# Spectral mixing with two channel networks on one core: two buffers for the first batch's second products, weight conversion as a list of operations, one group fewer multiplied unfolded, first pairs in two parts

## The chip, the cores and the metric

The kernel runs on 1 core of one Trainium2 chip. A core has five engines that run side by side, each with its own queue of instructions: TensorE (PE; matrix products), VectorE (DVE), ScalarE (ACT), GpSimd (POOL) and SyncE (SP), whose queue here only issues DMA transfers. ScalarE issues some too. The metric is the device time of one execution in microseconds (us); lower is better.

## The reference

Three layers follow each other on x of 4 batches x 3136 tokens x 256 channels, in fp32. The first is a filter along the sequence in the frequency domain; the second adds to its input the real part of a two-dimensional Fourier transform, and then a normalised two-layer network; the third is a network of the same kind with a gain.

```python
X = np.fft.rfft(x, axis=1)                      # first layer
x = np.fft.irfft(X * (filt_r + 1j * filt_i), n=3136, axis=1)
u = x + np.real(np.fft.fft(np.fft.fft(x, axis=1), axis=2))
un = (u - mean(u)) / np.sqrt(var(u) + 1e-6)     # second layer, over channels
x = u + np.maximum(un @ w1a, 0) @ w2a           # 256 -> 1024 -> 256
xn = (x - mean(x)) / np.sqrt(var(x) + 1e-6) * g # third layer
out = x + np.maximum(xn @ w1b, 0) @ w2b
```

## The kernel before

A sequence of 3136 is treated as 64 x 49: a transform of length 64 (`over_p`), one of length 49, the filter, and both back (`over_q`, 9 pairs j of frequency steps per batch). The channel transform is multiplied in when a block of tokens is prepared (`prep_ticks`). There are 25 blocks U of 512 tokens (the last 256); each goes through two network layers, and each layer is 8 steps m: `w1_step` (first product, 12 matrix instructions), `w1_evict` (ScalarE writes the high part `hh`, VectorE the low part `hl`), and `w2_step` (second product, 12 instructions). The products are exact to fp32 because each operand is split into a high and a low part and three products are added; so each weight has a high and a low part in SBUF.

The weights come as 64-bit words and are converted on the core, in chunks of 512 columns. A chunk goes through: load W (SyncE), masks E (two VectorE operations), value V (one, VectorE), scale A (two, ScalarE), join M (two, VectorE), high part H (ScalarE), low part L (VectorE). The first two chunks (w1a) are list A, tiles `we`; fourteen others are list Z, tiles `wm`, the first four of them w2a[0], w1a[1], w1a[3], w2a[1]. `conv_ticks` cuts this into ticks, with four chunks in work at a time.

The order of everything ahead of the first network step is written by hand: in `PLAN` each letter runs a tick of one stream (q: first batch's loop; a, c: conversion A and Z; p: preparation of block 0; x: x of batch 1; 0 to 3 and W to Z: transform of a group of batch 1, and its eviction). Behind that, `at` holds for each network step what runs in it, and `CONV` how many conversion ticks. An engine's queue is filled in the order of the code, and an engine executes it in that order; so an operation that waits holds up all behind it on its engine.

The loop of the first batch: for each j TensorE transposes g (L419) and multiplies (L251) into two banks R and I, VectorE multiplies them with the filter (first products y, L459; second products t2, L456), GpSimd adds the two (L461, L462) and forms z (L471, L472), TensorE transforms back (L251) and transposes (L506, L509), ScalarE evicts `vst` and `zt` and stores `vst`. Tile t2 has one buffer. Block 0's mixing begins on TensorE with the last `vst` (L659); it needs the whole loop. x of batch 1 is loaded in groups c of 512 KB. Groups 0 to 3 are multiplied whole (`whole_p`, 8 products of 512 columns on quarters of the array), the others are folded first: GpSimd forms sum and difference (L295, L296), 4 products follow (`over_p`).

Of the kernel before, what the change touches and what calls it, by code (L numbers as in the profile page):

```python
# [169 lines left out]
def spectral_mlp_kernel(ctx: ExitStack, tc, x, ff, cst, w1a, w2a, gln, w1b, w2b, out):  # L170
# [223 lines left out]
    def over_q(b):  # L394
# [32 lines left out]

        def into(j):
            g = g_raw.pop((b, j))
            R, I = (bank(2) for _ in range(2))  # L430
            f2 = const("f2")
            if j == 0:
                for r, o, n in ((0, R, "f2a"), (64, I, "f2a")):
                    quarter(o[:, 0], 0, const(n), r, NI, g[:, 0])
                for r, o, n in ((0, I, "f2b"), (64, R, "f2b")):
                    quarter(o[:, 0], 64, const(n), r, NI, g[:, 0])
# [343 lines left out]
    def conv_ticks(specs, bufs, when, lo_eng):  # L780

        chunks = []
        for n, j in specs:
            words = {"1a": w1a, "2a": w2a, "1b": w1b, "2b": w2b}[n].bitcast(I32).rearrange("p (n t) -> p n t", t=2)
            chunks.append((words, n, 512 * j))
        n = len(chunks)
# [2 lines left out]
        def load(t):
            for i in range(n):  # L790
                if when(i) != t:
                    continue
                words, _, a = chunks[i]
                ww[i] = bufs("w", i).bitcast(I32).rearrange("p (n t) -> p n t", t=2)
                nc.sync.dma_start(out=ww[i], in_=words[:, a:a + 512])

        load(-1)
        yield
        for t in range(n + LAG):
            load(t)  # L800
            i = t - LAG
            if i >= 0:
                _, name, a = chunks[i]
                dh, dl = (weight(name)[:, s].rearrange("p a b -> p (a b)") for s in range(2))
                conv_done.add(specs[i])
                split(vs.pop(i), dh[:, a:a + 512], dl[:, a:a + 512], lo_eng(i))
                yield
            i = t - 2
            if 0 <= i < n:
                p, v, w = ps.pop(i), vs[i], ww.pop(i)  # L810
                nc.vector.scalar_tensor_tensor(out=p, in0=w[:, :, 1], scalar=-0x80000000, in1=p,
                                               op0=ALU.bitwise_and, op1=ALU.bitwise_or)
                nc.vector.tensor_tensor(out=v, in0=v, in1=p.bitcast(F32), op=ALU.mult)
            i = t - 1
            if 0 <= i < n:
                nc.scalar.activation(out=ps[i], in_=ps[i], func=ACTF.Relu, scale=8.0, bias=-896.0 * 2 ** 23)
                nc.scalar.activation(out=vs[i], in_=vs[i], func=ACTF.Copy, scale=2.0 ** -20, bias=1.0)
            if 1 <= t <= n + 1:
                yield
            if t < n:  # L820
                low, high = ww[t][:, :, 0], ww[t][:, :, 1]
                e, m = (bufs(k, t).bitcast(I32) for k in "em")

                ps[t], vs[t] = e, m.bitcast(F32)
                nc.vector.tensor_single_scalar(out=e, in_=high, scalar=0x7FF00000, op=ALU.bitwise_and)
                nc.vector.tensor_single_scalar(out=m, in_=high, scalar=0xFFFFF, op=ALU.bitwise_and)
                yield
                nc.vector.scalar_tensor_tensor(out=vs[t], in0=low.bitcast(U32), scalar=2.0 ** -32, in1=m,
                                               op0=ALU.mult, op1=ALU.add)
                yield  # L830
# [338 lines left out]
```

## Time and profile before

| | us |
|---|---|
| median of 3 runs | 1345.01 (1344.9 to 1345.49) |
| profiled execution | 1344.32 |
| its span | 1342.5 |
| TensorE busy in the span | 1309.5 (98%) |
| VectorE, ScalarE, GpSimd busy | 783.9, 606.5, 257.6 |

The span is from the first to the last instruction of the profiled execution. Busy time of TensorE includes instructions that are in flight side by side, and their ends are modelled, so a busy TensorE may still lose time; its granted clock stands beside it. DMA moved 144.01 MB.

### The profile page before, as it was taken

The page shows a single profiled execution, that of the slowest core. Times are in us where ns is not written, and L with a number is a line of the kernel's source. Part 1 is how long each engine was busy: PE and PEld are TensorE (multiplying, and loading weights), DVE is VectorE, ACT ScalarE, POOL GpSimd, SP SyncE. Part 2 cuts the span into 40 slices and gives each one's busy share as a digit, 9 for nine tenths or more (in the row PEclk, how much of TensorE's full clock was granted, in tenths as well). Part 3 has the DMA queues.
Part 4 walks back from the last instruction along what each step waited for, and adds up shares of the span by engine and source line. Part 5 has one row for each costly group of instructions (what it writes and reads, how often), then busy time and mean ns, then how long its engine had stood idle before and what let it go on. Part 6 is the DMA issues. An engine that isn't in the chain of part 4 may idle for free.

```text
span 1342.5 us, 27955 instructions
## 1 busy us (share of the span) xinstructions
PE 1309.5 (98%) x11383; PEld 1213.0 (90%) x11383; DVE 783.9 (58%) x1633; ACT 606.5 (45%) x1142; POOL 257.6 (19%) x306
## 2 busy tenths in 40 slices
PE   7888999999999999999999999999999999999998
PEld 6467797989989989999989999999999999999998
DVE  5757775666555666656464665655545555565353
ACT  5455453454435444544435544545434543444222
POOL 2610202342230322212131231312000000000000
PEclk9988999999999999999999999999999999999999
DMA  7870222352544634623543635534222413432200
GB/s 246 308 245 17 67 86 83 117 164 81 149 130 133 159 91 113 170 53 95 129 132 106 165 104 119 151 82 107 56 64 48 95 41 71 79 85 43 63 17 25
DMA packets 209000, 144.01 MB, mean 107 GB/s; under 512 B 159196, under 2 KB 182492, under 8 KB 208872
## 3 DMA queue, kind: packets, MB, share of 16 engines
q1 hardware_dynamic: 192456, 112.20, 32.6%
q10 hardware_dynamic: 16416, 30.02, 5.9%
q8 instruction: 90, 1.47, 0.5%
q14 instruction: 38, 0.31, 0.1%
HBM read 83.08 MB, written 59.11 MB: 106 GB/s over the span
## 4 chain that ended last, share of the span: by engine, by line
PE 91%; DVE 4%; DMA 2%; ACT 1%; POOL 1%; issue 1%; SPq 0%; ACTq 0%; DVEq 0%
PE ps L869 40%; PE ps L842 39%; PE ps L251 7%; PE ps L664 3%; DMA fc<-in_ff 1%; PE ps L514 1%; PE ps L771 1%; DMA gd<-gst 1%; DVE t L456 1%; DVE y L459 1%; DMA ww<-in_w1a 0%; POOL y L462 0%; ACT xn L736 0%; DMA xr<-in_x 0%; PE ps L659 0%
## 5 line engine op out<-in xcount | busy, mean ns | idle before, releaser
L852 DVE SCALAR_TENSOR_TENSOR hl<-ps,hh 128x512 fp32r<-128x512 f32 (+1 forms) x400 | 269.7, 675 | 326.9 <-ACT hh L851 320.2
L851 ACT ACTIVATE hh<-ps 128x512 fp32r<-128x512 f32 (+1 forms) x400 | 233.9, 587 | 373.9 <-PE ps L869 330.6
L842 PE MATMUL ps<-xth,w1a 128*128 128x256 f32 x1568 | 244.9, 278 | 0.0
L842 PE MATMUL ps<-xth,w1b 128*128 128x256 f32 x1568 | 242.7, 276 | 0.0
L869 PE MATMUL ps<-w2a,hh 128*128 128x256 f32 x1568 | 220.8, 283 | 7.1 <-DVE w2a L248 4.0
L869 PEld LDWEIGHTS ps<-w2a,hh 128*128 128x128 f32 x1568 | 194.8, 189 | 35.8 <-issue 25.6
L869 PE MATMUL ps<-w2b,hh 128*128 128x256 f32 x1568 | 215.3, 279 | 0.0
L842 PEld LDWEIGHTS ps<-xth,w1a 128*128 128x128 f32 x1568 | 209.8, 189 | 1.4 <-ACT gst L359 1.4
L842 PEld LDWEIGHTS ps<-xth,w1b 128*128 128x128 f32 x1568 | 207.7, 188 | 0.0
L869 PEld LDWEIGHTS ps<-w2b,hh 128*128 128x128 f32 x1568 | 193.5, 188 | 13.7 <-issue 12.9
L719 POOL TENSOR_TENSOR rs<-rs,mhalf 128x4 f32<-128x4 f32 (+1 forms) x51 | 51.6, 1012 | 592.9 <-DVE rs L718 520.8
L842 PE MATMUL ps<-xtl,w1a 128*128 128x256 f32 x784 | 155.4, 278 | 0.0
L842 PE MATMUL ps<-xtl,w1b 128*128 128x256 f32 x784 | 154.2, 276 | 0.0
L730 ACT ACTIVATE xn<-u,nb,rs 128x256 f32<-128x256 f32 x148 | 117.1, 840 | 45.4 <-DVE nb L723 45.1
L869 PE MATMUL ps<-w2a,hl 128*128 128x256 f32 x784 | 122.5, 278 | 0.0
L869 PE MATMUL ps<-w2b,hl 128*128 128x256 f32 x784 | 121.6, 276 | 0.0
L842 PEld LDWEIGHTS ps<-xtl,w1a 128*128 128x128 f32 x784 | 119.7, 189 | 0.6 <-DVE xtl L765 0.6
L842 PEld LDWEIGHTS ps<-xtl,w1b 128*128 128x128 f32 x784 | 118.7, 188 | 0.0
L869 PEld LDWEIGHTS ps<-w2a,hl 128*128 128x128 f32 x784 | 104.8, 189 | 0.0
L869 PEld LDWEIGHTS ps<-w2b,hl 128*128 128x128 f32 x784 | 103.9, 188 | 0.0
L873 DVE TENSOR_TENSOR u<-ps,u 128x512 f32<-128x512 f32 x98 | 63.1, 684 | 44.0 <-PE ps L869 44.0
L461 POOL TENSOR_TENSOR y<-y,t 128x512 f32<-128x512 f32 (+1 forms) x35 | 43.5, 1243 | 148.8 <-DVE y L459 148.8
(133 smaller groups left out, 1422.1 us busy)
## 6 DMA issues: line engine op xcount, KB each, us to landing
xd<-xn SPq DMA_DIRECT2D x37, 512.0 KB
xtl<-xd SPq DMA_DIRECT2D x148, 128.0 KB
vd<-vst ACTq DMA_DIRECT2D x28, 512.0 KB
fc<-in_ff SPq DMA_DIRECT2D x26, 512.0 KB
vr<-vd SPq DMA_DIRECT2D x48, 256.0 KB
out<-u SPq DMA_DIRECT2D x24, 512.0 KB
xr<-in_x SPq DMA_DIRECT2D x18, 512.0 KB
gd<-gst ACTq DMA_DIRECT2D x36, 256.0 KB
```

The lines of the kernel that those rows point to most:

```text
L251: nc.tensor.matmul(out=o[c:c + 64], lhsT=lhs[r:r + k], rhs=rhs[r:r + k], **{"start": True, "stop": True, **kw})
L456: nc.vector.scalar_tensor_tensor(out=o[:, k], in0=i[:, k], scalar=sg[:, t:t + 1], in1=f[:, k, 1], op0=ALU.mult, op1=ALU.mult)
L459: nc.vector.tensor_tensor(out=o, in0=i[:, :n], in1=f[:, :n, a], op=ALU.mult)
L461: eng.tensor_tensor(out=y[:, :n, 1], in0=y[:, :n, 1], in1=t2[:, :n, 1], op=ALU.add)
L664: nc.tensor.matmul(out=ps[a][:, eo], lhsT=lhs, rhs=cs[eo][r], start=U > 0 and eo == 1 and i == 0, stop=False, skip_group_check=True)
L719: nc.gpsimd.tensor_tensor(out=rs[:, tl], in0=rs[:, tl], in1=mhalf[:, tl], op=ALU.pow)
L730: nc.scalar.activation(out=xs[t], in_=u[:, t].rearrange("p (k a j) -> p j k a", k=2, j=4), func=ACTF.Identity, scale=rs[:, t:t + 1], bias= ...
L842: nc.tensor.matmul(out=ps[:, c:c + 256], lhsT=w[:, a, k, m * 128:m * 128 + 128], rhs=xt[s][:, k, c:c + 256], start=i == 0, stop=i == len(t ...
L851: nc.scalar.activation(out=h[:, :n], in_=ps[:, :n], func=ACTF.Relu)
L852: nc.vector.scalar_tensor_tensor(out=l[:, :n], in0=ps[:, :n], scalar=0.0, in1=f32(h[:, :n]), op0=ALU.max, op1=ALU.subtract)
L869: nc.tensor.matmul(out=o[:, t % 2], lhsT=a[:, t * 128:t * 128 + 128], rhs=w[:, b, m], start=m == 0 and i == 0 and t % 2 == 0, stop=m == 7 ...
L873: nc.vector.tensor_tensor(out=u[:, t - 1:t + 1], in0=o, in1=u[:, t - 1:t + 1], op=ALU.add)
```

## The change

Seven things change.

1. In the first batch's loop second products have, for odd j, the two `zs` tiles as buffers of their own, for even j the old t2.
2. The conversion is a list of operations (`OPA`, `OPB`): each word is a tick, each pair a letter of the above and a chunk number. A chunk's E, V and A now come in one tick, M and H in one, L in one; each low part L of Z's later chunks follows the E, V, A of the next chunk.
3. Of batch 1's groups three are multiplied whole; group 3 is folded later, with the others. The third group is evicted at network step 1 (`call(1, early, "Y")`).
4. `PLAN` is another. x of batch 1 is loaded behind the last filter block instead of between the seventh and the eighth. The first chunks of Z come as E0 V0, E1 V1, A0 A1, E2 V2, M0 H0, M1 H1.
5. `vst`'s last three evictions in the first batch go to VectorE.
6. `CONV` spreads Z's ticks thinner, `P1` places batch 1's folded groups at other steps, `MID` its loop two steps later.
7. In batches 1 to 3 the first half of pair 0's product (`into0`) has a tick of its own ahead of the loop.

```diff
-DURING = {6: "a", 7: "a", 8: "a", 9: "a", 10: "a", 12: "a"}
-PLAN = "q qaq qaq qkq qaq qsq qxq qq qcq qcccq qcq qcqp qpp q ccp 0c1 p c2p c p x cWpp cc XY3Z"
-WHOLE = 4
-CONV = {0: 4, 1: 2, 2: 4, 3: 2, 4: 2, 5: 2, 6: 2, **{i: 1 + i % 2 for i in range(7, 28)}}
-P1 = (8, 10, 11, 13, 15, 17, 19)
-MID = 22
+DURING = {8: "a"}
+OPA = "W0W1 E0V0 E1V1 A0A1 M0H0 M1H1 L0 L1"
+OPB = "W0W1W2W3 E0V0 E1V1 A0A1 E2V2 M0H0W4 M1H1W5 L0W6 L1A2W7 M2H2 E3V3A3 L2"
+PLAN = "q a qq aqaq kqaq qaq qaq qsq qqx qcq qcq qcq qq pq cpcp qcc p 0c1W2 p cpc pp xXcc"
+WHOLE = 3
+CONV = {i: 1 + (i in (2, 4, 6)) for i in range(29)}
+P1 = (8, 9, 10, 12, 13, 15, 17, 18, 20)
+MID = 24
...
+        def into0():
+            g = g_raw[b, 0]
+            R, I = (bank(2) for _ in range(2))
...
-            t2 = tp.tile([128, 2, 2, D], F32, tag="t2", name="t2")
+            if own and j % 2:
+                t2 = [zsp.tile([128, 2, 4, 64], F32R, tag="zs" + e, name="t2").bitcast(F32) for e in "hl"]
+                t2 = [t.rearrange("p t q k -> p t (q k)")[:, :n] for t in t2]
+            else:
+                t2 = tp.tile([128, 2, 2, D], F32, tag="t2", name="t2")
+                t2 = [t2[:, :n, c] for c in range(2)]
...
-                    nc.scalar.activation(out=st[:, h:2 * n:2], in_=V[h][:, :n], func=ACTF.Copy)
+                    if own and j + h >= NDUO - 1:
+                        nc.vector.tensor_copy(out=st[:, h:2 * n:2], in_=V[h][:, :n])
+                    else:
+                        nc.scalar.activation(out=st[:, h:2 * n:2], in_=V[h][:, :n], func=ACTF.Copy)
...
+        opb = ops(OPB)
+        for t in range(4, len(Z) + 1):
+            more = t + 3 if t in (5, 6, 7) else t + 2
+            opb.append([("M", t - 1), ("H", t - 1)])
+            if t < len(Z):
+                opb.append([("E", t), ("V", t), ("A", t)] + [("W", more)] * (t in (5, 6, 7, 9, 10, 11)))
+            opb.append([("L", t - 1)])
...
+        call(1, early, "Y")
...
+            first(slots[0][0] - 1, q)
```

At the end of the first batch's loop VectorE's queue held this; L825 and L826 are E, L828 is V, of the first two chunks of Z, and `zsl` belongs to block 0's preparation:

```order
L461 TENSOR_TENSOR y<-y,t_734 128x256
L462 TENSOR_TENSOR y<-y,t_734 128x256
L825 TENSOR_SCALAR wm<-ww 128x512
L826 TENSOR_SCALAR wm<-ww 128x512
L828 SCALAR_TENSOR_TENSOR wm<-ww,wm 128x512
L825 TENSOR_SCALAR wm<-ww 128x512
L826 TENSOR_SCALAR wm<-ww 128x512
L828 SCALAR_TENSOR_TENSOR wm<-ww,wm 128x512
L616 TENSOR_TENSOR zsl<-zt,zsh 128x4x33 x2
```

Now it holds this (L814 and L815 are E, L818 is V, L509 is the eviction of `vst`):

```order
L473 TENSOR_TENSOR y<-y,t_736 128x256
L474 TENSOR_TENSOR y<-y,t_736 128x256
L814 TENSOR_SCALAR wm<-ww 128x512
L815 TENSOR_SCALAR wm<-ww 128x512
L818 SCALAR_TENSOR_TENSOR wm<-ww,wm 128x512
L509 COPY vst<-ps 128x2x256
L814 TENSOR_SCALAR wm<-ww 128x512
L815 TENSOR_SCALAR wm<-ww 128x512
L818 SCALAR_TENSOR_TENSOR wm<-ww,wm 128x512
L509 COPY vst<-ps 128x256 x2
L633 TENSOR_TENSOR zsl<-zt,zsh 128x4x33 x2
```

Three evictions of `vst` moved from ScalarE's queue into VectorE's, each behind a chunk's E and V; the one before `zsl` is the block with which the mixing begins.

Around the third network step, VectorE held this ahead of the low part of w2a[1] (L248, last row); L811 and L813 are M, L852 is `hl`, the two L248 rows between are w1a[3] and w2a[1]:

```order
L828 SCALAR_TENSOR_TENSOR wm<-ww,wm 128x512
L248 TENSOR_TENSOR w1a<-wm,w1a 128x512
L811 SCALAR_TENSOR_TENSOR wm<-ww,wm 128x512
L813 TENSOR_TENSOR wm<-wm 128x512
L852 SCALAR_TENSOR_TENSOR hl<-ps,hh 128x512
L825 TENSOR_SCALAR wm<-ww 128x512
L826 TENSOR_SCALAR wm<-ww 128x512
L828 SCALAR_TENSOR_TENSOR wm<-ww,wm 128x512
L248 TENSOR_TENSOR w2a<-wm,w2a 128x512
```

Now (L827 and L829 are M, L865 is `hl`, L836 is L):

```order
L633 TENSOR_TENSOR zsl<-zt,zsh 128x4x33 x2
L637 TENSOR_TENSOR zsl<-zt,zsh 128x4x31
L640 SCALAR_TENSOR_TENSOR zsl<-zt,con,zsh 128x4x31
L865 SCALAR_TENSOR_TENSOR hl<-ps,hh 128x512
L827 SCALAR_TENSOR_TENSOR wm<-ww,wm 128x512
L829 TENSOR_TENSOR wm<-wm 128x512
L865 SCALAR_TENSOR_TENSOR hl<-ps,hh 128x512
L814 TENSOR_SCALAR wm<-ww 128x512
L815 TENSOR_SCALAR wm<-ww 128x512
L818 SCALAR_TENSOR_TENSOR wm<-ww,wm 128x512
L836 TENSOR_TENSOR w2a<-wm,w2a 128x512
```

The chunk's M stands behind block 1's `zsl` and the `hl` of step 2, and its L behind the `hl` of step 3 and the next chunk's E and V.

On TensorE the first folded group of batch 1 (L251 `xf`) stood at network step 10, ahead of that step's second product:

```order
L869 MATMUL ps<-w2a,hh 128x256 x8
L869 MATMUL ps<-w2a,hl 128x256 x4
L842 MATMUL ps<-xth,w1a 128x256 x4
L842 MATMUL ps<-xtl,w1a 128x256 x2
L842 MATMUL ps<-xth,w1a 128x256 x4
L842 MATMUL ps<-xtl,w1a 128x256 x2
L251 MATMUL ps<-xf,con 64x512 x4
L869 MATMUL ps<-w2a,hh 128x256 x8
```

Now it stands one pair of products earlier, at step 9 (and is group 3 instead of group 4):

```order
L882 MATMUL ps<-w2a,hh 128x256 x8
L882 MATMUL ps<-w2a,hl 128x256 x4
L855 MATMUL ps<-xth,w1a 128x256 x4
L855 MATMUL ps<-xtl,w1a 128x256 x2
L855 MATMUL ps<-xth,w1a 128x256 x4
L855 MATMUL ps<-xtl,w1a 128x256 x2
L252 MATMUL ps<-xf,con 64x512 x4
L882 MATMUL ps<-w2a,hh 128x256 x8
```

The rows around it read alike; what moved is the place of the `xf` row, which the program order counts from the start of the network steps: eight second products (steps 0 to 7) and one more (step 8) stand ahead of it now, ten before. On GpSimd the group's fold follows block 2's `zmid` of step 8 in both.

## Rows read from the trace of the kernel before

**Rows 1.** Busy time by stretch: us, busy (count) of each engine, granted clock, DMA share, GB/s

```profile
40.00:60.00 20.00, 18.19 (x136) 9.91 (x137) 15.38 (x30) 11.28 (x24) 15.25 (x17) 1.00 0.99 356
66.00:76.00 10.00, 8.00 (x52) 6.49 (x56) 4.32 (x10) 5.59 (x15) 1.24 (x2) 0.83 0.70 237
76.00:140.00 64.00, 54.24 (x399) 44.72 (x392) 46.52 (x98) 33.69 (x69) 10.58 (x11) 0.89 0.32 110
140.00:160.00 20.00, 17.87 (x140) 14.60 (x138) 12.48 (x30) 10.66 (x21) 2.37 (x2) 0.91 0.16 54
160.00:1342.50 1182.50, 1176.74 (x10401) 1111.84 (x10399) 676.12 (x1411) 523.89 (x979) 212.00 (x250) 1.00 0.37 98
```

**Rows 2.** Timeline of TensorE: start, duration, operation, count [idle before, what ended it]

```profile
21.83 1.39 PE L419 MATMUL ps<-con,gt 128*114 128x128 f32 x11 [1.45 <-DVE gt L334]
...
68.00 5.30 PE L659 MATMUL ps<-vst,cr 128*128 128x256 f32 x16 [2.69 <-ACT vst L496]
...
75.53 5.33 PE L251 MATMUL ps<-xr,con 64*64 64x512 f32 x48
...
84.98 3.68 PE L251 MATMUL ps<-xr,con 64*64 64x512 f32 x16 [1.24 <-ACT gst L359]
...
94.93 1.93 PE L869 MATMUL ps<-w2a,hh 128*128 128x256 f32 x8 [1.83 <-ACT hh L851]
...
105.48 1.23 PE L869 MATMUL ps<-w2a,hh 128*128 128x256 f32 x4 [1.20 <-DVE w2a L248]
...
111.93 1.19 PE L869 MATMUL ps<-w2a,hh 128*128 128x256 f32 x8
...
118.14 0.74 PE L869 MATMUL ps<-w2a,hh 128*128 128x256 f32 x4 [2.63 <-DVE w2a L248]
...
137.18 2.07 PE L251 MATMUL ps<-xf,con 64*64 64x512 f32 x8
...
152.35 0.33 PE L771 MATMUL ps<-con,xn 128*128 128x128 f32 x1 [1.78 <-ACT xn L736]
```

**Rows 3.** VectorE's groups, 20 to 66 us: busy, mean ns, idle before

```profile
L456 DVE SCALAR_TENSOR_TENSOR t<-ps,con,fc 128x256 f32<-128x256 f32 x34 | 14.9, 476 | 4.2 <-POOL y L462 4.1
L459 DVE TENSOR_TENSOR y<-ps,fc 128x512 f32<-128x512 f32 (+1 forms) x18 | 11.7, 651 | 4.8 <-PE ps L251 2.4 <-DMA fc<-in_ff 2.3
...
L813 DVE TENSOR_TENSOR we<-we 128x512 f32<-128x512 f32 x2 | 2.3, 1168 | 0.1
```

**Rows 4.** Timeline of VectorE, first batch's loop

```profile
24.31 0.69 DVE L459 TENSOR_TENSOR y<-ps,fc 128x512 f32<-128x512 f32 x1 [1.38 <-PE ps L251]
...
56.87 0.69 DVE L459 TENSOR_TENSOR y<-ps,fc 128x512 f32<-128x512 f32 x1 [2.34 <-DMA fc<-in_ff]
...
63.34 0.68 DVE L825 TENSOR_SCALAR wm<-ww 128x512 int32<-128x512 int32 x1
```

**Rows 5.** Timeline of GpSimd: sums of j = 0 and 7, first fold

```profile
26.46 1.27 POOL L461 TENSOR_TENSOR y<-y,t 128x512 f32<-128x512 f32 x1 [24.35 <-DVE y L459]
...
59.02 1.27 POOL L461 TENSOR_TENSOR y<-y,t 128x512 f32<-128x512 f32 x1 [1.86 <-DVE y L459]
...
134.70 1.75 POOL L295 TENSOR_TENSOR xf<-xr 128x512 f32<-128x512 f32 x1
```

**Rows 6.** Timeline of SyncE's issues, x of batch 1

```profile
41.79 2.68 SPq L287 DMA_DIRECT2D xr<-in_x  x4
```

**Rows 7.** Timeline of VectorE at network steps 1 and 2

```profile
101.43 0.68 DVE L811 SCALAR_TENSOR_TENSOR wm<-ww,wm 128x512 int32<-128x512 int32 x1
...
103.35 0.42 DVE L825 TENSOR_SCALAR wm<-ww 128x512 int32<-128x512 int32 x1
...
104.74 0.68 DVE L248 TENSOR_TENSOR w2a<-wm,w2a 128x512 fp32r<-128x512 f32 x1
```

**Rows 8.** Timeline of ScalarE at network step 0

```profile
94.28 1.09 ACT L851 ACTIVATE hh<-ps 128x512 fp32r<-128x512 f32 x2 [0.48 <-ACT gst L359]
...
96.70 0.40 ACT L638 ACTIVATE zmid<-zsh 128x256 fp32r<-128x256 f32 x1
```

More of the change, by code (lines that the diff above doesn't have):

```diff
@@ L401, in over_q @@
         lag = 2 if own else 1
+        part = []
         ys, zs, vst = {}, {}, {}
@@ L426, in store @@
             nc.scalar.dma_start(out=dst, in_=vst.pop(j)[:, :k1 - k0])
+        def into0():
+            g = g_raw[b, 0]
+            R, I = (bank(2) for _ in range(2))
+            for r, o, n in ((0, R, "f2a"), (64, I, "f2a")):
+                quarter(o[:, 0], 0, const(n), r, NI, g[:, 0])
+            for r, o, n in ((0, I, "f2b"), (64, R, "f2b")):
+                quarter(o[:, 0], 64, const(n), r, NI, g[:, 0])
+            return R, I
         def into(j):
+            R, I = part.pop() if part else into0() if j == 0 else [bank(2) for _ in range(2)]
             g = g_raw.pop((b, j))
-            R, I = (bank(2) for _ in range(2))
             f2 = const("f2")
             if j == 0:
[L433 to L436, printed above, removed]
                 for r, o in ((0, R), (64, I)):
@@ L460, in filt @@
             eng = side(j)
-            eng.tensor_tensor(out=y[:, :n, 1], in0=y[:, :n, 1], in1=t2[:, :n, 1], op=ALU.add)
-            eng.tensor_tensor(out=y[:, :n, 0], in0=y[:, :n, 0], in1=t2[:, :n, 0], op=ALU.subtract)
+            eng.tensor_tensor(out=y[:, :n, 1], in0=y[:, :n, 1], in1=t2[1], op=ALU.add)
+            eng.tensor_tensor(out=y[:, :n, 0], in0=y[:, :n, 0], in1=t2[0], op=ALU.subtract)
             ys[j] = y
@@ L554, in over_q @@
         sign(0)
+        yield
+        part.append(into0())
         yield
@@ L778, in ln_ticks @@
             yield
[L780 to L786, printed above, removed]
-        ww, ps, vs = {}, {}, {}
[L789 to L830, printed above, removed]
@@ new lines, in conv_ticks, with parts, load, masks @@
+    def conv_ticks(specs, bufs, ticks):
+        ww, ps, vs = {}, {}, {}
+        def parts(i):
+            name, j = specs[i]
+            return [weight(name)[:, s].rearrange("p a b -> p (a b)")[:, 512 * j:512 * j + 512] for s in range(2)]
+        def load(i):
+            name, j = specs[i]
+            words = {"1a": w1a, "2a": w2a, "1b": w1b, "2b": w2b}[name].bitcast(I32).rearrange("p (n t) -> p n t", t=2)
+            ww[i] = bufs("w", i).bitcast(I32).rearrange("p (n t) -> p n t", t=2)
+            nc.sync.dma_start(out=ww[i], in_=words[:, 512 * j:512 * j + 512])
+        def masks(i):
+            e, m = (bufs(k, i).bitcast(I32) for k in "em")
+            ps[i], vs[i] = e, m.bitcast(F32)
+            nc.vector.tensor_single_scalar(out=e, in_=ww[i][:, :, 1], scalar=0x7FF00000, op=ALU.bitwise_and)
+            nc.vector.tensor_single_scalar(out=m, in_=ww[i][:, :, 1], scalar=0xFFFFF, op=ALU.bitwise_and)
+        def value(i):
+            nc.vector.scalar_tensor_tensor(out=vs[i], in0=ww[i][:, :, 0].bitcast(U32), scalar=2.0 ** -32,
+                                           in1=vs[i].bitcast(I32), op0=ALU.mult, op1=ALU.add)
+        def scale(i):
+            nc.scalar.activation(out=ps[i], in_=ps[i], func=ACTF.Relu, scale=8.0, bias=-896.0 * 2 ** 23)
+            nc.scalar.activation(out=vs[i], in_=vs[i], func=ACTF.Copy, scale=2.0 ** -20, bias=1.0)
+        def join(i):
+            p = ps.pop(i)
+            nc.vector.scalar_tensor_tensor(out=p, in0=ww.pop(i)[:, :, 1], scalar=-0x80000000, in1=p,
+                                           op0=ALU.bitwise_and, op1=ALU.bitwise_or)
+            nc.vector.tensor_tensor(out=vs[i], in0=vs[i], in1=p.bitcast(F32), op=ALU.mult)
+        def high(i):
+            nc.scalar.activation(out=parts(i)[0], in_=vs[i], func=ACTF.Copy)
+        def low(i):
+            h, l = parts(i)
+            nc.vector.tensor_tensor(out=l, in0=vs.pop(i), in1=f32(h), op=ALU.subtract)
+            conv_done.add(specs[i])
+        does = {"W": load, "E": masks, "V": value, "A": scale, "M": join, "H": high, "L": low}
+        for tick in ticks:
+            for op, i in tick:
+                does[op](i)
+            yield
@@ L931, in spectral_mlp_kernel, with ops @@
              ("1", "b", (1, 3)), ("2", "b", (1, 2, 3)))))
-        cv = conv_ticks(A, bufs_a, lambda i: -1, lambda i: nc.vector)
+        def ops(text):
+            return [[(w[k], int(w[k + 1])) for k in range(0, len(w), 2)] for w in text.split()]
+        cv = conv_ticks(A, bufs_a, ops(OPA))
         for c in range(9):
@@ L984, in spectral_mlp_kernel @@
                 nx += 1
-            elif what in "0123WXYZ":
+            elif what in "012WXY":
                 early(what)
@@ L990, in spectral_mlp_kernel @@
         run(p)
-        nc_ = PLAN.count("c")
-        left = 2 + 4 * len(Z) - nc_
+        left = len(opb) - PLAN.count("c")
         blocks = [(0, 0)]
```

9 lines of the change are left out of this document (4 added, 5 removed).

## The prediction

> **What bounds the kernel now.** I read the busy time by stretch first [rows 1]. From 160 us to the end TensorE is busy 1176.74 of 1182.50 us at clock 1.00, so a microsecond won or lost ahead of 160 us arrives whole at the end, and the question is only what lies ahead. There TensorE is busy 8.00 of 10, 54.24 of 64 and 17.87 of 20 us, 13.9 us idle, and its mean granted clock is 0.83, 0.89 and 0.91: 1.7 + 7.0 + 1.8 = 10.5 us lost to the lower of its two levels (1.2 instead of 2.4 GHz). The stretch 66 to 76 holds one wait, 2.69 us ahead of the first mixed product [rows 2], and loses 1.7 us of clock behind it; the stretch 76 to 140 holds four such places (84.98, 94.93, 105.48, 118.14) and 7.0 us, 140 to 160 one (152.35) and 1.8 us. So a place where TensorE waits some 2 us costs its wait and 1.7 us more.
>
> Second, who ends these waits [rows 2]: the last result block `vst` (68.00), ScalarE's eviction of `gst` (84.98) and of `hh` (94.93), VectorE's low part of a converted weight (105.48, 118.14), the normalised tokens `xn` (152.35). Third, the loop of the first batch ahead of 66 us, on VectorE, GpSimd and SyncE [rows 3 to 6]: it runs in steps of (59.02 - 26.46) / 7 = 4.65 us [rows 5], VectorE idles 4.2 us ahead of second products, nearly all for GpSimd, and 4.8 us ahead of first ones, 2.3 of it for a filter block that SyncE issued behind four x blocks [rows 3, 6].
>
> **The loop and the start of the mixing.** In the first stage VectorE's copies of the first transform have three conversion operations between them instead of six. The 1.45 us wait at 21.83 [rows 2] shrinks to about 0.5: the loop starts at 23.4 instead of 24.31 [rows 4]. From there VectorE needed 39.0 us to the first conversion behind the loop (63.34), with 4.2 + 4.8 - 1.4 (the idle time ahead of 24.31 itself) = 7.6 us of idle time [rows 3, 4]. All of that is what two buffers and filter loads ahead of x can take away. Added in the loop is the first chunk's M pair, which stood ahead of it: the two L813 took 2.3 us, 0.7 outside the loop and 1.6 in it, so I price the pair at 2.8 us there. VectorE alone would then end at 23.4 + 39.0 - 7.6 + 2.8 = 57.6; with only the filter wait gone, at 62.9. I take 58 to 60.
>
> What is late next is weights. x and W are now issued behind the last filter blocks, about 9.3 us ahead of the loop's end (two and a half steps of VectorE's work), at 48.3; before, x went out at 41.79 [rows 6]. Up to the second W stand half a block of filter, 3 of x and 2 of W, plus 3 stores of `vst`: 8.5 blocks of 524 KB at the 356 GB/s of the saturated stretch 40 to 60 [rows 1] are 12.5 us, so it lands at 60.8, with a fourth store 62.3. VectorE's order now puts E, V (three operations) of chunk 0, a `vst` copy, E, V of chunk 1 and two copies ahead of the first mixed product: E and V took 1.4 us [rows 7], the first copy 0.6 and the two 256-wide ones 0.7 I estimate by the 0.7 of L248 there and half of it. From 61.1 that gives 63.2, against 68.00: **gain 4.8 us**. TensorE, whose last transposes I put at 60.6, then still waits 2.6 us, so the clock falls as before. Bounds: weights in time give 57.6 + 1.4 + 0.6 + 1.4 + 0.7 = 61.7 and a wait too short for the clock, 6.3 + 1.7 = 8.0; a loop that ends at 62.9 gives 67, gain 1.0. ScalarE gives up three copies; its A pairs move behind all of that.
>
> **From the mixing to step 10.** In times of before (75.53 the x products, then 4.8 earlier by the above). Group 3 leaves: its 8 products took 3.68 us at the low clock [rows 2], 1.8 at the high one by the 24 that took 5.33. ScalarE now evicts one group ahead of `xn` and A, H of chunk 2 between, so the first product of the first layer can start at 84.0 instead of 84.98 + 3.68 = 88.66. `hh` no longer stands behind four groups' evictions and their stores, so the second layer starts at 88.1 instead of 94.93, without its 1.83 us. Then the gain is spent:
> At the third second-layer step the low part of chunk 3 is needed. Its chain: two `hh` to 88.1, `zsh` to `zmid` 1.8 us (95.37 to 97.10 [rows 8]), `hh` 90.5, `hl` 91.2, M 92.5, H 93.1, then the third group's eviction and store issue 1.65, `hh` 95.25, `hl` 95.9, E, V 97.2, L 97.8. TensorE stands there from 94.2, 3.7 us (before 1.25 + 1.20), and goes on at 97.8 instead of 105.48. At the fifth step, low part of chunk 4: 8 + 12 products and the mixing of block 1 take 6.45 us (105.48 to 111.93) and end at 104.3; before, L then came 6.1 us later, now E, V of chunk 5 stand ahead of it and it is 6.9: 111.2 instead of 118.14, a wait of 3.7 instead of 2.63. At the seventh it is 8.9 us later, 120.1.
> Then the folded group 3. Its products stand at step 9, those of the first folded group before at step 10 (TensorE's order in the section on the change); the fold itself stands in both behind `zmid` on GpSimd, and that behind VectorE's `zsl`, now behind E, V of chunk 7. I put `zmid` at 130.2, the fold's two operations, 1.75 us each as the one at 134.70 [rows 5] less a little, at 133.2, and TensorE at that place from 127.8: 5.0 us wait and 1.7 of clock. Behind it, two more layer steps end at 138.1, where before stood 137.18 + 2.07 = 139.25: of the 6.9 us **1.0 is left**. Bounds: each of the four waits (3.7, 3.7, 0.6, 5.0) may be off by 1 us: -3 to +5.
>
> **Steps 11 to 13 and the rest.** Ahead of the 1.78 us wait at 152.35 stand now the products of the next folded group, and between VectorE's `rs` and `nb` `hl` and L instead of M, `hl` and E, 1.2 us less. Some wait stays, too short for the clock: **gain 2.1** of 1.78 + 0.3 + 1.7 = 3.8; bounds 0 to 3.8. One more folded group is to be multiplied: 4 products, half of 1.78: **loss 0.9**. The first pair of batches 1 to 3 in two parts are the same products a step earlier; they hide under the nothing-idle stretch behind 160, and the g blocks are loaded three steps ahead; if a PSUM bank were lacking, each time one step's eviction would show. I cost them at nothing, as the positions of batch 1's ticks.
>
> Sum: 4.8 + 1.0 + 2.1 - 0.9 = 7.0. The profiled execution took 1344.32 us, 1342.5 of it the span; less 7.0 that is 1337.3. The median of the runs is 1345.01, 0.7 above it: 1338.0.
>
> **Rivals.** *Weights in time*: if the transfers end some 2 us earlier, W is no bound, the clock stays up at the mixing, and the first term is 8.0: 1334.8. For it: SyncE's loads compete with three stores only.
> *Weights later*: from 41.79 to 56.87, four x blocks and one filter block, 2.6 MB, passed SyncE's queue, 174 GB/s of the 356 [rows 1, 4, 6]. At that rate 2.9 MB take 16.5 us, W lands at 64.8, and the first term is 1.1: 1341.7. Against it: the stores come from steps of 3 to 4 us and do not fill their half. The Trainium skill, DMA: Bandwidth & Descriptors, section Queues, rings and completion order, says that each DMA engine takes turns between the queues that have work; by that rule this would be the case as long as stores are queued, and the row agrees with it for the stretch of before.
> *VectorE and GpSimd shut each other out*: two buffers let GpSimd's sums meet VectorE's conversions more often. The row for it is L813, 0.7 us alone and 1.6 in the loop [rows 3]. If every conversion and every sum met, the steps would stay at 4.65 us, the loop would end at 62.9, the first term would be 1.0: 1341.8. The Trainium skill, SBUF — State Buffer, section SBUF: two separate sides, calls that port pair an exclusive lock: a VectorE operation with two SBUF inputs and a GpSimd operation run one after the other. The rule speaks against this change; the filter products read PSUM and one SBUF input, so it would touch the conversions only, and L813 agrees.
> *Slower*: ScalarE and VectorE hand chunks to each other in a fixed order from step 0 to 8, each standing in its queue behind the other's. If the four waits there come to 23 us instead of 13, the kernel loses 3: 1348. The waits of before there (1.25 + 1.20, 2.63, 0.18) speak against so much.
> *Nothing*: the loop's pace is TensorE's own work and the gain stays below 2.7 us.
>
> **Numbers.** The forecast (1335.5 to 1340.5) 0.45; weights in time or a better steps 0 to 13 0.25; weights later 0.08; shut out 0.07; steps 0 to 10 worse by 3 to 5 us, or nothing, 0.10; slower 0.05. A measurement of this kernel tells some 0.2% (2.7 us) from no change: faster below 1342.3. That holds for the first four cases but a part of the third and fourth: 0.80; same 0.14; slower 0.06. Range 1332.5 to 1343.
>
> **What would show it.** No wait for the filter block on VectorE in the loop and steps near 4.1 us; the mixing at 63 with a wait of 2 to 3 us ahead; no wait for `hh` or `gst`; waits for low parts of 3 to 4 us; a new wait for GpSimd's `xf` at step 9; none over 1 us at block 2's `xn`. Wrong it would be if W's landing is not what holds the mixing, or if the low parts come on time.

## The result, and the profile after

The changed kernel is slower: median 1353.53 us of 7 runs (1349.15 to 1358.0) against 1345.01 of 7 (1344.29 to 1345.91), ratio 1.0063 (95% interval 1.0042 to 1.0083). Forecast were 1338.0, with 0.06 for slower. The profiled execution took 1353.19 us, its span 1351.3 against 1342.5. From here on a ratio is to the kernel before, timed on the same chip, and ratios are turned into microseconds with 1345.

First the busy time by stretch of the changed kernel, as in [rows 1], with 160 to 250 us apart.

```profile
0.00:66.00 66.00, 51.60 (x405) 35.40 (x405) 48.07 (x89) 33.84 (x67) 32.37 (x42) 0.97 0.77 267
66.00:76.00 10.00, 9.70 (x56) 7.56 (x60) 6.46 (x15) 4.59 (x10) 1.16 (x2) 0.70 0.63 192
76.00:140.00 64.00, 49.41 (x365) 41.37 (x358) 39.74 (x89) 31.33 (x61) 10.31 (x11) 0.90 0.33 117
140.00:160.00 20.00, 16.55 (x138) 14.01 (x138) 11.25 (x27) 8.64 (x17) 3.51 (x3) 0.99 0.14 44
160.00:250.00 90.00, 87.10 (x723) 79.69 (x723) 60.48 (x130) 43.00 (x86) 17.34 (x21) 0.96 0.33 104
250.00:1351.00 1101.00, 1097.10 (x9701) 1036.74 (x9700) 621.15 (x1291) 484.51 (x901) 194.62 (x229) 1.00 0.38 97
```

Behind 250 us TensorE idles 3.9 us at clock 1.00, in the kernel before 3.8; the loss lies ahead of it. Lower clock costs 2.0 + 3.0 + 6.4 + 0.2 + 3.6 = 15.2 us (each stretch times what its granted clock lacks to 1), 10.5 before; TensorE idles 14.6 us in 76 to 140, where it was 9.8 [rows 1].

Next TensorE's timeline of the changed kernel, to be laid beside [rows 2]; only rows with waits that matter here, and the first x products (75.04).

```profile
33.05 1.16 PE L521 MATMUL ps<-con,y 128*128 128x128 f32 x8 [3.35 <-ACT gr L422]
...
66.30 6.52 PE L676 MATMUL ps<-vst,cr 128*128 128x256 f32 x16 [4.28 <-ACT zsh L636]
...
75.04 5.33 PE L252 MATMUL ps<-xr,con 64*64 64x512 f32 x48
...
97.98 0.72 PE L882 MATMUL ps<-w2a,hh 128*128 128x256 f32 x4 [3.56 <-DVE w2a L836]
...
111.55 0.73 PE L882 MATMUL ps<-w2a,hh 128*128 128x256 f32 x4 [3.63 <-DVE w2a L836]
...
121.10 0.73 PE L882 MATMUL ps<-w2a,hh 128*128 128x256 f32 x4 [1.31 <-DVE w2a L836]
...
132.75 1.31 PE L252 MATMUL ps<-xf,con 64*64 64x512 f32 x4 [3.67 <-POOL xf L296]
134.42 1.97 PE L252 MATMUL ps<-xf,con 64*64 64x512 f32 x4 [0.36 <-POOL xf L297]
...
153.68 0.33 PE L788 MATMUL ps<-con,xn 128*128 128x128 f32 x1 [0.46 <-ACT xn L753]
...
159.80 0.73 PE L855 MATMUL ps<-xth,w1a 128*128 128x256 f32 x4 [2.49 <-ACT xth L248]
```

The forecast waits for low parts and for `xf` are there and those for `hh` and `gst` are gone. Two were not forecast: 33.05 in the loop and 159.80 in step 14. What releases them stands in ScalarE's timeline of the changed kernel.

```profile
31.89 0.63 ACT L832 ACTIVATE w1a<-we 128x512 fp32r<-128x512 f32 x1 [5.22 <-DVE we L829]
32.42 1.06 ACT L422 ACTIVATE gr<-ps 114x512 f32<-114x512 f32 x2
...
158.63 0.63 ACT L832 ACTIVATE w2b<-wm 128x512 fp32r<-128x512 f32 x1 [2.08 <-DVE wm L829]
...
159.17 1.06 ACT L248 ACTIVATE xth<-ps 128x512 fp32r<-128x512 f32 x2
```

The reader is to see one pattern twice: the high part H (L832) waits for VectorE's join M (L829) of the same tick, and the eviction that TensorE needs (`gr`, `xth`) stands behind it. Such a step from one engine to the other is called a hand-over below. The Trainium skill, TensorE: Matmul & The Clock Gate, section Architectural detail: the array is 16× 32×32, not 1× 128×128, says that ScalarE and VectorE take their queues strictly first in, first out; both rows agree. How much of it there is shows the view of ScalarE's waits, 20 to 260 us (us in total, times, longest):

```profile
ACT wm L822 <- DVE wm L814: 14.1, 11, 3.1
...
ACT w2b L832 <- DVE wm L829: 9.9, 4, 2.9
...
ACT w1b L832 <- DVE wm L829: 9.0, 4, 2.4
ACT w1a L832 <- DVE we L829: 8.7, 2, 5.2
...
ACT w2a L832 <- DVE wm L829: 6.2, 3, 2.1
```

That is 33.8 us of waiting for joins in 13 places; the same view of the kernel before has 3.5 us for its high parts (L247: 2.3, 0.8, 0.4), because H came three ticks behind M there.

The clearest ledger is when TensorE begins the second product of a network step (its first instruction with `hh`). Differences are to before; the runs e3, e7 and e9 are told below. Each column is one execution.

| step | before | changed | difference | e3 | e7 | e9 |
|---|---|---|---|---|---|---|
| 0 | 94.93 | 88.36 | -6.57 | -5.10 | -6.46 | -3.49 |
| 8 | 131.64 | 126.20 | -5.44 | -8.16 | -5.43 | -5.10 |
| 9 | 134.36 | 136.32 | +1.96 | -0.82 | -5.43 | -5.10 |
| 13 | 156.81 | 155.68 | -1.13 | -4.72 | -3.36 | -4.19 |
| 15 | 162.38 | 167.00 | +4.62 | -1.73 | -3.15 | -3.41 |
| 28 | 200.34 | 205.77 | +5.43 | -1.62 | -0.11 | -1.35 |
| 35 | 229.49 | 235.90 | +6.41 | -1.64 | +0.85 | -1.38 |
| 36 | 234.69 | 242.70 | +8.01 | -0.03 | +0.85 | -1.28 |

So the lead at step 0 lives until step 8; only 0.5 us of it come from the loop and the mixing (the x products start at 75.04 instead of 75.53), the rest from what lies between them and step 0. It is lost at step 9 (7.4 us: the fold) and between 13 and 36 (9.1 us).

### The profile page after: what moved, and what is told of

It reads as the page before. It is cut to its first block, busy times and chain, and to the rows that moved or that the text cites. A ratio compares the mean times of both kernels' runs of the same rounds, so it can differ in the third digit from the quotient of the medians.

```text
span 1351.3 us, 27946 instructions
## 1 busy us (share of the span) xinstructions
PE 1311.5 (97%) x11375; PEld 1214.8 (90%) x11375; DVE 787.1 (58%) x1636; ACT 605.9 (45%) x1139; POOL 259.3 (19%) x308
## 4 chain that ended last, share of the span: by engine, by line
PE 89%; DVE 5%; ACT 2%; DMA 2%; issue 1%; POOL 0%; SPq 0%; ACTq 0%; DVEq 0%; POOLq 0%
PE ps L882 39%; PE ps L855 37%; PE ps L252 8%; PE ps L681 3%; DMA xr<-in_x 1%; DMA ww<-in_w2a 1%; PE ps L529 1%; DVE hl L865 1%; PE ps L788 1%; ACT xn L753 1%; PE ps L676 0%; DVE xtl L782 0%; ACT hh L864 0%; DVE wm L818 0%; PE ps L421 0%
## 5 line engine op out<-in xcount | busy, mean ns | idle before, releaser
L865 DVE SCALAR_TENSOR_TENSOR hl<-ps,hh 128x512 fp32r<-128x512 f32 (+1 forms) x400 | 270.1, 676 | 343.5 <-ACT hh L864 332.8
```

The costliest lines, as they stand in the source:

```text
L865: nc.vector.scalar_tensor_tensor(out=l[:, :n], in0=ps[:, :n], scalar=0.0, in1=f32(h[:, :n]), op0=ALU.max, op1=ALU.subtract)
```

## Experiments

**e1: the fold ahead of the casts.** The numbers of `P1` are the network steps at which the ticks of batch 1's groups run; the first is group 3's fold, the second its products.

```diff
-P1 = (8, 9, 10, 12, 13, 15, 17, 18, 20)
+P1 = (7, 9, 10, 12, 13, 15, 17, 18, 20)
```

> The changed kernel with one number of P1 changed: the fold of group 3 of batch 1 is issued at step 7 and no longer at step 8, so that on GpSimd it stands ahead of the casts of block 2's middle row (L657), for which GpSimd waits until 130.5 us. Theory A (the change's own waits cost what they last, and each brings some 1.7 us of lower clock): the waits of 3.7 and 0.4 us ahead of group 3's product at 132.75 go, and with them the low clock of 133 to 141 us (3.2 us by the granted clock): 6 to 7 us less than the changed kernel, about 1347, ratio to the kernel before near 1.001. Theory B (the wait covers another that ends at nearly the same time, such as block 2's normalisation at step 13, which waited 1.8 us in the kernel before): under 3 us less, about 1351.

Measured 1.0027 (1.0017 to 1.0036), 4.8 us less than the changed kernel: between the two. The wait at step 9 is gone, but another has grown. VectorE's timeline of this run, then GpSimd's:

```profile
107.73 1.64 DVE L818 SCALAR_TENSOR_TENSOR wm<-ww,wm 128x512 f32<-128x512 uint32 x1
109.29 1.22 DVE L740 SCALAR_TENSOR_TENSOR nb<-mv,rs 128x4 f32<-128x4 f32 x1
```

```profile
107.56 1.26 POOL L296 TENSOR_TENSOR xf<-xr 128x512 f32<-128x512 f32 x1
108.79 1.71 POOL L297 TENSOR_TENSOR xf<-xr 128x512 f32<-128x512 f32 x1
```

In the changed kernel the same two VectorE operations take 0.69 and 0.16 us; here the first ends 0.55 us after the fold's first operation and the second together with the fold's second, and the low part behind them lets TensorE stand 5.64 us at 111.17 instead of 3.63. The Trainium skill, SBUF — State Buffer, section SBUF: two separate sides, calls the port pair of VectorE and GpSimd an exclusive lock; these four rows agree.

**e7: the folded groups' products a step later, group 3's at step 10.**

```diff
-P1 = (8, 9, 10, 12, 13, 15, 17, 18, 20)
+P1 = (8, 10, 11, 13, 14, 16, 18, 19, 21)
```

> The changed kernel with P1 a step later from its second entry on: group 3's product of batch 1 runs at step 10, as a group of the same kind does in the kernel before, and no longer at step 9. The fold stays behind the casts on GpSimd, so it doesn't meet VectorE earlier, unlike in the run with the fold at step 7. Theory A (fold too late for step 9): the wait of 4.0 us and its 3.2 us of low clock go, 5 to 7 us less than the changed kernel, about 1347, and more than the 4.4 us that the fold at step 7 gave, since the slowing of VectorE at 107 to 111 us is not bought with it. Theory B (any wait removed at step 9 is found again in waits at steps 13 and 14): 3 us or less.

Measured 1.0008 (0.9999 to 1.0017), 7.4 us less than the changed kernel. TensorE's timeline of this run:

```profile
132.86 1.08 PE L252 MATMUL ps<-xf,con 64*64 64x512 f32 x4 [1.05 <-POOL xf L296]
134.53 1.08 PE L252 MATMUL ps<-xf,con 64*64 64x512 f32 x4 [0.60 <-POOL xf L297]
...
148.81 0.33 PE L788 MATMUL ps<-con,xn 128*128 128x128 f32 x1 [2.18 <-ACT xn L753]
```

The fold ends when it did, TensorE has one step more to do till then, and the products run at the high clock (1.08 instead of 1.31 and 1.97 us). Theory A by the size, but not by the place where it is won. By the ledger, of the 7.4 us at step 9 only 2.2 are left at step 13: group 3's products now come behind step 9's start, and TensorE waits 2.18 us for `xn` instead of 0.46, as theory B had it. Then 5.5 us are won between steps 13 and 15, where the wait of 2.49 us for `xth` is gone, though H stands where it stood. ScalarE's timeline of this run, then TensorE's:

```profile
152.79 0.63 ACT L832 ACTIVATE w2b<-wm 128x512 fp32r<-128x512 f32 x1 [2.08 <-DVE wm L829]
153.32 1.07 ACT L248 ACTIVATE xth<-ps 128x512 fp32r<-128x512 f32 x2
```

```profile
151.54 1.99 PE L252 MATMUL ps<-xf,con 64*64 64x512 f32 x8
```

ScalarE waits the same 2.08 us for the join with `xth` behind it. But the products of the next folded group, which the changed kernel has a step earlier (149.20), now keep TensorE busy until `xth` is there. So the places of the groups were worth about what the whole change lost, and the wait at 159.80 needed both: H right behind its join, and the group a step early.

**e2: H0 and H1 a position later in the loop.**

```diff
-OPA = "W0W1 E0V0 E1V1 A0A1 M0H0 M1H1 L0 L1"
+OPA = "W0W1 E0V0 E1V1 A0A1 M0 M1H0 H1L0 L1"
```

> The changed kernel with ScalarE's two high parts of the first chunks (H0, H1) each issued one position later in the loop of batch 0 than VectorE's join (M0, M1), so that they no longer hold up the evictions of the next sums. Theory A (hand-over): TensorE's wait of 3.35 us at 33.05 and the 1.7 us of low clock behind it go, the loop ends 4 to 5 us earlier, the weights are asked for earlier too, and the time falls by 3 to 5 us, to about 1349. Theory B (the end of the loop is set by the landing of the weights at 62 and 64 us, which doesn't move): the loop is faster but the mixing still starts at 65 to 66 us, and the time falls by less than 1 us.

Measured 1.0056 (1.0042 to 1.0069): 0.9 us less, not told from nothing. The wait of 3.35 us is gone (two of 1.2 to 1.3 us stand in the loop instead), the loads of weights go out 1 us earlier (49.82 instead of 50.81), and the mixing starts at 64.82 instead of 66.30; at step 3 1.2 us of it are left, at step 36 0.9. Theory B by the size, though the landing of the weights moved too.

**e8: the two copies ahead of the masks.**

```diff
-PLAN = "... qqx qcq qcq qcq qq pq ..."
+PLAN = "... qqx qcq qq qcq qcq pq ..."
```

> The changed kernel with the masks of the chunks E0 and E1 moved behind the two last copies of VectorE in batch 0 (vst, L509), which stood behind them while VectorE waited for the weights' landing at 61.9 us. Theory A: the store and the last eviction behind the copy on ScalarE come 2 us earlier, the mixing starts near 64 instead of 66.3, and with less low clock the time falls by 2 to 3 us. Theory B (what follows waits for the later of the two anyway: low parts at 97.98 to 121.10 come from the conversion, which doesn't move): under 1 us.

Measured 1.0041 (1.0026 to 1.0056): 3.0 us less by the ratios, whose intervals overlap; its profiled execution was no faster than that of the changed kernel (1353.9 and 1353.19). The mixing starts at 65.23 instead of 66.30. What it removes is seen in VectorE's timeline of the changed kernel:

```profile
61.93 0.43 DVE L814 TENSOR_SCALAR wm<-ww 128x512 int32<-128x512 int32 x1 [2.59 <-DMA ww<-in_w2a]
...
63.34 0.68 DVE L509 COPY vst<-ps 128x512 f32<-128x512 f32 x1
64.38 0.43 DVE L814 TENSOR_SCALAR wm<-ww 128x512 int32<-128x512 int32 x1 [0.35 <-DMA ww<-in_w1a]
```

The copy stood behind masks that waited for weights, a store on ScalarE behind the copy, and the last `zt` and `zsh` behind the store. Theory A had the mixing start near 64; what holds the copies next are earlier stores of `vst`, as VectorE's timeline of e8 has it:

```profile
61.60 0.69 DVE L509 COPY vst<-ps 128x512 f32<-128x512 f32 x1 [1.48 <-DMA vd<-vst]
...
64.70 0.76 DVE L509 COPY vst<-ps 128x256 f32<-128x256 f32 x2 [1.01 <-DMA vd<-vst]
```

**e3: H a tick behind its join, from the fourth chunk on.**

```diff
-            opb.append([("M", t - 1), ("H", t - 1)])
+            opb.append([("M", t - 1)])
             if t < len(Z):
-                opb.append([("E", t), ("V", t), ("A", t)] + ...)
+                opb.append([("H", t - 1), ("E", t), ("V", t), ("A", t)] + ...)
```

> The changed kernel with the high part H of each chunk from the fourth on moved out of the tick of its join M into the next tick, ahead of the next chunk's masks. Theory A: ScalarE no longer waits 2.1 us for VectorE with evictions queued behind it; TensorE's wait of 2.5 us for xth at 159.8 and its 1.7 us of low clock go: 3 to 4 us less, about 1350. Theory B (the waits for the low parts at 97.98, 111.55 and 121.10 decide; they get longer because the low part now waits for a later H): no gain or up to 4 us more, 1353 to 1357.

Measured 0.9982 (0.9974 to 0.9991): 10.9 us less than the changed kernel, more than A expected, and faster than before. It doesn't act in one place: by the ledger, 2.7 us are won to step 8, 0.9 to step 13, 2.8 between 13 and 15 and 1.7 from there to step 36. The low parts didn't come later, as B had it, but earlier. TensorE's waits for them in this run, where 97.98, 111.55 and 121.10 stood:

```profile
97.03 0.72 PE L882 MATMUL ps<-w2a,hh 128*128 128x256 f32 x4 [1.15 <-DVE w2a L836]
...
109.02 1.22 PE L882 MATMUL ps<-w2a,hh 128*128 128x256 f32 x4 [3.52 <-DVE w2a L836]
...
118.20 0.74 PE L882 MATMUL ps<-w2a,hh 128*128 128x256 f32 x4 [1.21 <-DVE w2a L836]
```

**e12: the same cost put into the kernel before.** High part moved from the split into the tick of the join:

```diff
-                split(vs.pop(i), dh[:, a:a + 512], dl[:, a:a + 512], lo_eng(i))
+                lo_eng(i).tensor_tensor(out=dl[...], in0=vs.pop(i), in1=f32(dh[...]), op=ALU.subtract)
...
                 nc.vector.tensor_tensor(out=v, in0=v, in1=p.bitcast(F32), op=ALU.mult)
+                nc.scalar.activation(out=dh[...], in_=v, func=ACTF.Copy)
```

> The kernel before with the suspected cost put in: ScalarE's high part of each chunk is issued right behind the join of the same chunk, as in the changed kernel, and no longer a tick later; L keeps its place. Theory A (ScalarE waits some 2 us for VectorE with evictions queued behind it): new waits of TensorE for xth or hh or vst of 1 to 3 us at a few places, 3 to 8 us slower, ratio 1.002 to 1.006. Theory B (the hand-over is hidden, and the run with H later gained through something else): within 1.5 us of the kernel before.

Measured 1.0146 (1.0133 to 1.0160): 19.6 us slower, two and a half times the upper end of A. TensorE's waits in this run (us in total, times, longest), 20 to 260 us:

```profile
PE ps L771 <- ACT xn L736: 8.3, 8, 4.3
PE ps L872 <- DVE w2a L806: 6.1, 3, 3.0
PE ps L872 <- ACT hh L854: 3.6, 4, 1.1
PE ps L506 <- ACT gr L420: 3.2, 1, 3.2
```

The pair e3 and e12 shows this cause both ways: taking it out of the one kernel wins 11 us, putting it into the other loses 20. Here A stands behind the waiting H as well, and the first chunks in the loop are changed too, so the amount is not that of the change.

**e5: low part ahead of the next masks.** The two `append` lines of `[("E", t), ...]` and `[("L", t - 1)]` change places.

> The changed kernel with the low part L of each chunk from the fourth on issued ahead of the next chunk's masks, value and scaling, not behind them. Theory A: TensorE's waits of 3.56, 3.63 and 1.31 us for the low parts of the second layer's weights come from the place of L behind E, V and A in VectorE's queue (H was done at 93.2, L began at 97.24); with L first they shrink to under 1 us each and two stretches of low clock of 1.7 us go: 8 to 11 us less, about 1344. Theory B (the conversion as a whole is late, so that the next chunk's join is late by as much as the low part gains): under 4 us less, about 1350.

Measured 1.0010 (1.0002 to 1.0019): 7.1 us less, between the two theories. The waits for low parts shrink from 8.5 to 3.8 us, less than A had, and `xth` and `xn` take part of it back.

**e6: e3, and L behind the next masks in their tick.**

```diff
+                opb.append([("H", t - 1), ("E", t), ("V", t), ("L", t - 1), ("A", t)] + ...)
+                opb.append([])
```

> The changed kernel with H apart from its join, as in the run with the high part later, and the low part L now right behind the next chunk's masks and value in the same tick (the third tick of each chunk is empty, so the joins keep their places). Theory A: both the waits for low parts and those for xth go, the gains of the two runs (10 and 7 us against the changed kernel) add in good part: about 1340, ratio 0.996. Theory B (the two runs removed the same waits, with the wait for the fold left as it is): no better than the better of the two, 1343 to 1345.

Measured 0.9980 (0.9972 to 0.9989), as e3: theory B by the size. That e3 and e5 remove the same delay fits this, but e6 is not the two edits together (L stands behind the next masks, not ahead of them), so it isn't shown.

**e13: the scaling A a tick behind its masks, alone.**

```diff
-                opb.append([("E", t), ("V", t), ("A", t)] + ...)
-            opb.append([("L", t - 1)])
+                opb.append([("E", t), ("V", t)] + ...)
+            opb.append([("L", t - 1)] + [("A", t)] * (t < len(Z)))
```

> The changed kernel with the scaling A of each chunk from the fourth on moved out of the tick of its masks into the next tick, beside the low part of the chunk ahead; H stays with its join. Theory A (every hand-over from VectorE to ScalarE within a tick costs, since ScalarE's evictions stand behind it): 2 to 5 us less than the changed kernel, 1349 to 1352. Theory B (the waits for masks, 1.3 us each, are hidden, only those for joins of 2 to 3 us reach TensorE): within 1.5 us of the changed kernel.

Measured 1.0018 (1.0007 to 1.0029): 6 us less, above A's range. So this hand-over costs something too, as long as the first is there (e14).

**e4: the two buffers alone.** Part 1 of the change in the kernel before.

> The kernel before with one part of the change alone: two buffers in turn for the second products of batch 0. Theory A (as in the prediction): VectorE no longer waits 4.2 us for GpSimd in the loop, the steps shorten to some 4.1 us, the mixing starts 2 to 4 us earlier, and about 2 to 4 us of it are left at the end: 1341 to 1343. Theory B (the end of the loop and of the whole is set by weights, folds and later waits, which take it back): within 1 us of the kernel before.

Measured 0.9984 (0.9974 to 0.9993), 2.2 us faster. TensorE's timeline of this run, beside 68.00 and 94.93 of [rows 2]:

```profile
64.85 5.41 PE L664 MATMUL ps<-vst,cr 128*128 128x256 f32 x16 [1.93 <-ACT vst L501]
...
92.64 2.02 PE L874 MATMUL ps<-w2a,hh 128*128 128x256 f32 x8 [2.56 <-ACT hh L856]
```

3.15 us are won at the mixing, 2.3 at the start of step 0's second product, 2.2 at the end by the ratio. Theory A by the ratio. This trace alone doesn't show the end: it is of an execution of 1345.15 us, above the run's median of 1342.74, its lead is still 2.1 us at step 13 and gone at step 36.

**e9, e10, e11, e14, e15: edits together.** e9 is e3 and e7. e10 adds e2 and e8. e11 takes e6's tail for e3's and gives steps 0 and 1 two ticks (`CONV = {i: 1 + (i in (0, 1, 2, 4, 6)) ...}`). e14 is e9 with A a tick later, e15 is e11 with A in the empty tick.

> The changed kernel with two edits together: H of each chunk from the fourth on a tick behind its join (alone 10 us less than the changed kernel), and group 3's product at step 10 (alone 7.4 less). Theory A (two separate causes, and without them the change does what the prediction said): the gains add nearly in full, 14 to 17 us less, 1337 to 1340 where the kernel before has 1346, ratio 0.993 to 0.996. Theory B (both edits remove the same stretch of lower clock and waits between 130 and 165 us): no more than the better one, 1343 to 1344, ratio 0.998.

> The same two edits and, with them, H0 and H1 a position later in the loop (alone 0.9 us less, not told from nothing) and the two copies ahead of the masks E0 and E1 (alone 3 us less). Theory A: the loop's wait of 3.35 us at 33 is worth its time only if the end of the loop doesn't wait for masks; now it doesn't, so 3 to 6 us less than with the two edits, 1332 to 1336. Theory B (the waits for the low parts of the second layer's weights, which hang on the landing of the weights' words and on VectorE, take it back): within 1.5 us of the run with two edits.

> The four edits, with L behind the next masks in the same tick, and two ticks of the conversion in steps 0 and 1 of the first layer where the changed kernel has one, so that chunks 3 to 5 are joined half a step to a step earlier. Theory A: the waits for low parts (5.9 us in the run with H later, and 1.7 us of lower clock) shrink below 2 us: 3 to 5 us less than with the four edits. Theory B (VectorE is too full in steps 0 to 2, the low halves of the hidden rows come later): no gain or a loss of up to 3 us.

> The run with two edits undone (H a tick later, group 3 at step 10; ratio 0.9964) and A a tick later as well. Theory A: 2 to 4 us less again, ratio 0.993 to 0.995. Theory B: within 0.1% of 0.9964.

> The run with earlier ticks and all edits (ratio 0.9953) with A in the third, empty tick of each chunk. Theory A: the waits for xn (10.2 us in that run, the longest 4.0) and low clock shrink, 2 to 4 us less, ratio 0.992 to 0.994. Theory B: within 0.1% of 0.9953, or worse because the next join now comes close behind its scaling.

| run | ratio | 95% interval |
|---|---|---|
| e9 | 0.9964 | 0.9951 to 0.9977 |
| e10 | 0.9952 | 0.9938 to 0.9965 |
| e11 | 0.9953 | 0.9941 to 0.9965 |
| e14 | 0.9965 | 0.9954 to 0.9977 |
| e15 | 0.9939 | 0.9927 to 0.9951 |

e9 is 13.3 us below the changed kernel where the two edits alone gave 10.9 and 7.4: three quarters of the sum, nearer to A. e10 and e11 aren't told from it or from each other, though in e11 no wait for a low part is left among TensorE's waits; what it wins there comes back as waits for `xn`, the longest 4.0 us. e14 equals e9: with the join's hand-over and the fold undone, the masks' one is hidden (B). e15, median 1337.06 (1336.47 to 1337.53), has the lowest ratio of the study, in theory A's range and 8 us below the kernel before; its interval overlaps with those of e9, e10 and e11.

## Why the prediction was wrong

By its own terms, against the ledger and TensorE's timeline, ahead is positive:

| stretch | forecast | measured | short by |
|---|---|---|---|
| to the x products (75.53, now 75.04) | 4.8 | 0.5 | 4.3 |
| from there to step 10 (139.18, now 141.01) | 1.0 | -2.3 | 3.3 |
| steps 11 to 13 (156.81, now 155.68) | 2.1 | 3.0 | -0.9 |
| all behind | -0.9 | -9.9 | 9.0 |
| sum (rounded singly) | 7.0 | -8.8 | 15.8 |

**The step that failed** is the last sentence of the sum's working: the first pairs in two parts and "the positions of batch 1's ticks" were costed at nothing, and the ticks of the conversion behind step 8 got no term at all. The first pairs alone no run tests; the positions and the ticks do cost, and 9.0 of the 15.8 us lie behind step 13. There the hand-over of H went on, and with the groups a step early it reached TensorE: the wait of 2.49 us at 159.80 with its 1.7 us of low clock is the largest. Of the 7.5 us that are lost between steps 13 and 35, e3 wins 4.5, e7 3.3 and both together (e9) 4.7, so these are not two separate costs. Another 1.6 are lost between 35 and 36, for which no edit need be blamed (last section). The argument for nothing was that TensorE has no idle time behind 160; but that was a fact of the kernel before, in which H stood three ticks behind M and the groups stood at other steps.

**The rival that came true** was named, but in the wrong place and at 0.05: ScalarE and VectorE standing in their queues behind each other. It was put into steps 0 to 8 with 23 us of waits instead of 13; there the waits are 3.56 + 3.63 + 1.31 + 4.03 = 12.5, as forecast. Its price lay in the loop and, for the most part, behind step 8 (of what e3 wins, 2.7 us lie ahead of step 8).

**To the x products.** That the loop would start earlier (forecast 23.4, VectorE's first product came at 22.89) and lose its wait for filter blocks was right. Missed was the 3.35 us at 33.05 with 1.7 of low clock; mis-sized the landing of the second W, 64.4 instead of 60.8 to 62.3. That is nearly the rival *weights later* (0.08), which had the landing at 64.8 and a first term of 1.1: the 2.9 MB that it counts up to the second W took from 48.81 to 64.38, some 185 GB/s of the 352 GB/s that the DMA moved in that time. Each of e2 and e8 gives 1.1 to 1.5 us at the mixing; in e15, which has both, it starts at 64.24. Behind the start the mixing costs more than before: it starts 1.7 us earlier and the x products 0.5, with the granted clock in 66 to 76 at 0.70 instead of 0.83.

**To step 10.** Waits for low parts of 3.7, 3.7 and 0.6 were forecast, 3.56, 3.63 and 1.31 came. The fold's wait was forecast with 5.0 and 1.7 of clock; it came with 4.0, but the granted clock was 0.67 over 130 to 140 us, 3.3 us lost. The mechanism was right; mis-sized were the clock, by 1.6 us, and the end of the fold: GpSimd's second operation ended at 134.37 (0.5 more in the times of before), not at 133.2, 1.7 us later, and TensorE itself came later too, so that the wait was not longer. What I had not asked was whether the step could be had for nothing one position later (e7).

**Steps 11 to 13.** Right in kind: 0.46 us are left of the 1.78, and the clock stays up (0.99 in 140 to 160); 3.0 us came instead of 2.1.

**Buffers.** Right in kind: e4 gives 2.2 us at the end by the ratio. Shutting out of VectorE and GpSimd (0.07) happened, but in few places. It shows in e1, and in the changed kernel in the loop: the first chunk's join, for which H waits 5.22 us at 31.89, took 1.76 and 1.56 us while GpSimd's sums ran, where 0.7 each is the time alone. How much of the 3.35 us at 33.05 this makes, no run separates.

Not accounted for singly are some 3 us of the 9.0 behind step 13; e9 still loses 2.9 us from step 13 to 36, 0.9 of them the extra group by the forecast's price.

## What to carry to other kernels

When two engines hand a value back and forth, put the consumer a tick behind the producer in the consumer's queue: the wait isn't paid by the value but by whatever stands behind it, and the profile of the kernel before can't show it. When a list of operations is rewritten, cost each hand-over at each place where it occurs, those in quiet stretches above all, since a busy engine is only busy as long as what feeds it keeps its order. A step that starts as soon as its input is ready is worth trying one position later. And a wait that two edits can each remove belongs to neither alone: run them singly and together.
